# Last stage of a gated mix of long convolution and dilated attention: wider tiles, column groups, and a new order

## The chip, the cores and the metric

One core of a Trainium2 chip runs the program. The metric is device time in microseconds (us), the median of several runs. PE is TensorE, DVE is VectorE, ACT is ScalarE, POOL is GpSimd, SP is the engine that issues most transfers (DMAs).

## The reference, cut to what matters

```python
g = sigmoid((x * gate_w).sum(-1, keepdims=True))        # x = A_q, 2048 rows of 640
kv = short_conv4(A_k, A_shift_k) * A_v
a = x * (long_conv(kv, A_ssm_k) + kv * A_ssm_D)         # causal, length 2048, by FFT
q, k, v = split(x @ B_wqkv)                             # 32 heads of 20
o = softmax over 8 keys at distance 0, 2, ..., 14
out = g * a + (1 - g) * (o @ B_wo)
```

The attention branch works on the same x = A_q. All inputs and the output are bf16.

## The kernel before

Rows are split by parity. x is loaded, transposed on PE (L467) and projected: v (`vproj`, psv, L528) and q, k (`qkproj`, pj, L575) into staging tiles, from which POOL's transfers (`fragger`, L614) build per-group tiles qb, kb of four heads. For each of eight groups of heads PE makes scores (L636), ACT their exponentials (L643), PE the weighted sums O (L664), and DVE divides (L673, L676) into oS. Meanwhile DVE makes the short convolution (`conv`, L481 to L488) and the product with v (L492).

The long convolution is a two-step transform of the kernel h and of u = kv: s1 (`s1_unit`, L697) and s2 (`s2_unit`, L713), in two halves P of 20 + 22 units each in all, with every unit copied out of PSUM by ACT (L284) or DVE (L286). `swaps` (L805, L807) moves halves of h across partitions by DMA into Hw. `products` (L751) multiplies in the transform domain on DVE. `inverse1` (L820) makes 20 units of the first inverse step. `op_tr` (L838) transposes oS, `outproj` (L854) projects it in 16 steps of 128 rows by 640 columns, and the copy out scales it by 1 - g (L858). `load_q` loads x again in the output's layout (L873). `final` does the second inverse step: for each group of three rows t (and a last of one), 32x32 tiles of the matrix T on PE (L893), six ACT copies of 320 scaled by g (L901), then on DVE a multiply by q (L906), an add of the projected attention (L908), and four stores on SP (L911).

The order of all this is set at build time. Each part is a generator that yields requests; a planner (`Plan`) holds a clock for each engine, picks the request with the earliest modelled start plus a weight per part (`PRI`), and chooses ACT or DVE for copies, with leanings (`LEAN_*`). What it picks is issued in that order on each engine; engines run in order and wait on semaphores. Four PSUM slots are shared by all PE work.

Of the kernel before, what the change touches and what calls it, by code (L numbers as in the profile page):

```python
# [17 lines left out]
S = 2048  # L18
# [30 lines left out]
BG = 1266.0  # L49
# [6 lines left out]
def fft_consts():  # L56
# [24 lines left out]
    T = np.tile(T.reshape(32, 64 * 2 * 32), (4, 1))  # L81
# [49 lines left out]
class Req:  # L131


    def __init__(self, engs, cost=0.0, deps=(), take=0, give=(), n=0, move=0.0, pri=None, mode=None, bg=None, mm=0, lean=0.0):
        self.engs, self.cost, self.deps, self.take, self.give, self.n, self.move = engs, cost, deps, take, give, n, move
        self.pri, self.mode, self.bg, self.mm, self.lean = pri, mode, bg, mm, lean
# [4 lines left out]
LEAN_QK = -248.0  # L141
LEAN_V = 87.0
LEAN_H = -137.0
PRI = dict(loads=0, fragger=0, xpose=-9.2, score_gen=-8.6, pv_gen=-5.7, conv=-1.6, conv_v=-24.1, bulk=0, conv_end=0, qkproj=-4.2, vproj=-4.8,
           gate=-0.8, load_G=0, h_slot=0, p2_slot=10.2, u_slot=0, swaps=0, load_T=0, op_tr=4.7, outproj=37.5, load_q=0, products=6.3, final=-18.6,
           h_stream=(-3.7, -4.9), u_stream=(0.9, 2.5), inverse1=(33.7, 30.7))
# [4 lines left out]
class Plan:  # L151


    def __init__(self, nslots):
        self.at = dict(P=0.0, A=0.0, D=0.0, G=0.0, S=0.0, Q=0.0)
# [6 lines left out]
        self.lane = {"S": lane, "Q": lane, "G": []}  # L162
        self.slots = [Bank() for _ in range(nslots)]
        self.streams = []
        self.log = []

    def add(self, gen, pri):
        self.streams.append([pri, gen, next(gen)])
# [6 lines left out]
    def start(self, r, e):  # L175
        t = self.at[e]
        if e == "P" and r.mode != self.mode:
            t += SWITCH
        for d in r.deps:
            if d.t is None:  # L180
                return INF
            t = max(t, d.t + LAT.get((d.eng, e), 60.0))
# [9 lines left out]
    def best(self, r):  # L192
        found = []
        for e in r.engs:
            s = self.start(r, e)
            found.append((s + self.cost(r, e) + (r.lean if e == "A" else 0.0), s, e))
        end, s, e = min(found)
        return s + self.cost(r, e) if s < INF else INF, s, e

    def run(self):  # L200
        while self.streams:
            pick = None
            for k, (pri, gen, r) in enumerate(self.streams):
                end, st, e = self.best(r)
                if st == INF:
                    continue
                p = pri if r.pri is None else r.pri
# [5 lines left out]
            pri, gen, r = self.streams[k]  # L213
# [16 lines left out]
            self.at[e] = end  # L230
# [19 lines left out]
            try:  # L250
                self.streams[k][2] = gen.send(g)
            except StopIteration:
                del self.streams[k]
# [3 lines left out]
def kernel(  # L257
# [45 lines left out]
    g_nat = p0.tile([128, 16], F32, name="g_nat")  # L303
    omg = p0.tile([128, 16], F32, name="omg")
# [62 lines left out]
    def loads():  # L367
# [9 lines left out]
        for c in (1, 0):  # L377
            for q in range(4):
                yield from load(f"k{q}{c}", kin[32 * q:32 * q + 32, 3 + 32 * c:35 + 32 * c, :],
                                raw(k2, 32 * c * D + QC * q, [[64 * D, 32], [D, 32], [1, QC]]), 2000.0)  # L380
        for c in range(2):
            for q in range(4):
                yield from paced(f"v{q}{c}", vin[32 * q:32 * q + 32, c], raw(v2, QC * q + 80 * c, [[64 * D, 32], [D, 64], [1, 80]]), 2100.0)
        yield Req("S", 1.0, [ev("xtr")])
        h_lin = p0.tile([128, 80, 2, 64], BF, name="h_lin", tag="HL")
        st["h_lin"] = h_lin
        for P in range(2):
            for q in range(4):
                for c in range(2):
                    yield from paced(f"h{P}{q}{c}", h_lin[32 * q:32 * q + 32, PL * P:PL * P + PL, c, :],  # L390
                                     raw(A_ssm_k, (160 * q + 80 * c + PL * P) * S, [[64, 32], [S, PL], [1, 64]]), 1200.0)
# [12 lines left out]
    def load_G():  # L404
        yield Req("S", 1.0, [ev("conv"), ev("grow"), ev("vproj")])
# [9 lines left out]
    def load_T():  # L415
        yield Req("S", 1.0, [ev("p2")])
# [3 lines left out]
        yield Req("S", 1.0, [ev("hw1")])  # L420
        T = st["p2"].tile([128, 64, 2, 32], BF, name="T")
        st["T"] = T
        yield from load("T", st["T"][:], cf["T"].ap().rearrange("p (a r b) -> p a r b", a=64, r=2), 2700.0)
# [6 lines left out]
    def heads():  # L430
# [14 lines left out]
        for q in range(4):  # L445
            nc.gpsimd.dma_start(Dz[32 * q:32 * q + 1, :], raw(A_ssm_D, 160 * q, [[0, 1], [1, 160]]))
        for e in range(2):
            masks(e)
            if e == 0:
                for q in range(4):  # L450
                    nc.gpsimd.memset(kin[32 * q:32 * q + 1, 0:3, :], 0.0)
                    nc.gpsimd.dma_start(wraw[32 * q:32 * q + 32].rearrange("p c j -> p (c j)"), raw(A_shift_k, 4 * QC * q, [[0, 32], [1, 4 * QC]]))
        for q in range(4):
            for a, b in ((1, 17), (17, 32)):
                nc.gpsimd.dma_start(kin[32 * q + a:32 * q + b, 0:3, :], raw(k2, (64 * a - 3) * D + QC * q, [[64 * D, b - a], [D, 3], [1, QC]]))
# [59 lines left out]
    def conv_end():  # L515
        g = yield Req("G", 1.0, [ev("convV")])
        mark("conv", g)

    def vproj():
        for n in range(NB):  # L520
# [9 lines left out]
            r = yield Req("AD", n=640, deps=[g.done], give=g.banks, lean=LEAN_V)  # L530
# [5 lines left out]
    def gate():  # L536
# [12 lines left out]
        for gg in range(4):  # L549
            r = yield Req("S", 500.0, [r.done] if gg == 0 else [], move=200.0)  # L550
            nc.sync.dma_start(g_nat[32 * gg:32 * gg + 32, :], raw(src, 64 * (gg % 2) * pt + 16 * (gg // 2), [[32 * pt, 2], [32, 16], [1, 16]]))
        mark("grow", r)
        r = yield Req("D", 500.0, [Ev(r.done.t + 5000.0), ev("conv")])
# [7 lines left out]
    def qkproj():  # L561
        free = [None] * NSTG
        for ft in range(NDT):
            for w in range(2):
# [4 lines left out]
                for k in range(3):  # L569
# [9 lines left out]
                    r = yield Req("AD", n=2 * m, deps=deps, give=g.banks, lean=LEAN_QK)  # L579
# [14 lines left out]
    def fragger():  # L594
# [4 lines left out]
        for ft in range(NDT):  # L599
            for w in range(2):  # L600
                yield Req("G", 1.0, [ev(f"pj{ft}{w}")])
# [84 lines left out]
    def s1_unit(key, P, oc, Am):  # L686
# [14 lines left out]
        e = yield Req("AD", n=1024, deps=[r.done], give=r.banks, lean=LEAN_H if key == "h" else 0.0)  # L701
# [4 lines left out]
    def s2_unit(key, j0, n, Am, deps):  # L706
# [9 lines left out]
        e = yield Req("AD", n=320 * n, deps=[r.done], give=r.banks, lean=LEAN_H if key == "h" else 0.0)  # L716
# [6 lines left out]
    def transform(key, P):  # L723
# [5 lines left out]
        outs = []  # L729
        for j0, n in JS:  # L730
            pdone, edone = yield from s2_unit(key, j0, n, Am, evs)
            outs.append(edone)
            if key == "u":
                todo.append((P, j0, n, edone))
                at(f"todo{len(todo)}", 0.0)
        x = ev(f"{key}s2{P}")
        x.t, x.eng = pdone.t, pdone.eng
        for k, o in enumerate(outs):
            x = ev(f"{key}{P}out{k}")
            x.t, x.eng = o.t, o.eng  # L740

    todo = []

    def products():
        for k in range(2 * len(JS)):
            yield Req("D", 1.0, [ev(f"todo{k + 1}")])
            P, j0, n, edone = todo[k]
            for key in "hw":
                r = yield Req("D", 150.0 + 0.53 * 320 * n, [edone, ev(f"hw{P}")])
                X, U = [st[(x, P)][:].rearrange("p c o (q j) l -> p c (o q) (j l)", j=32)[:, :, :, 4 * j0:4 * j0 + 4 * n] for x in (key, "u")]  # L750
                nc.vector.tensor_tensor(X, U, X, ALU.mult)  # L751
            if k % len(JS) == len(JS) - 1:
                mark(f"mult{P}", r)
# [4 lines left out]
    def h_slot():  # L758
        for P in range(2):
            yield Req("G", 1.0, [ev(f"h{P}{q}{c}") for q in range(4) for c in range(2)])  # L760
            g = yield Req("G", 600.0, [Ev(max(x.t for x in [ev(f"h{P}{q}{c}") for q in range(4) for c in range(2)]) + 6000.0)])
# [4 lines left out]
    def p2_slot():  # L766
        yield Req("G", 1.0, [ev("qk"), ev("gatePE"), ev("frags"), ev("grow")])
# [6 lines left out]
    def h_stream(P):  # L774
        yield Req("G", 1.0, [ev(f"Dz{P}"), ev("p2" if P else "SX")])
        yield from transform("h", P)

    def u_slot():
        yield Req("G", 1.0, [ev("pv"), ev("oS"), ev("p2")])
# [11 lines left out]
    def u_stream(P):  # L791
        yield Req("G", 1.0, [ev("p3"), ev("conv")])
        yield from transform("u", P)

    def swaps():
        for P in range(2):
            yield Req("S", 1.0, outs("h", P) + [ev("p3")] + ([ev("us10"), ev("us11")] if P else []))
# [13 lines left out]
    def inverse1(P):  # L811
        yield Req("G", 1.0, [ev(f"mult{P}")])
# [15 lines left out]
    def op_tr():  # L828
        yield Req("G", 1.0, [ev("oS"), ev("hs10"), ev("hs11")])
# [14 lines left out]
    def outproj():  # L844
        yield Req("G", 1.0, [ev("oTall"), ev("wo"), ev("gate")])
        bl = p0.tile([128, 16, D], BF, name="bl", tag="oS")
        st["bl"] = bl
        wo, oT = st["wo"], st["oT"]
        for t in (*range(4, 16), *range(4)):
            g = yield Req("P", 5 * (215.0 + 56.0), [ev(f"oT{ft}") for ft in range(NDT)], take=1, mode="f", mm=10)  # L850
            op = psum(g, "op", (128, 1024))
            for ft in range(NDT):
                for n0, n1 in ((0, 512), (512, 640)):
                    nc.tensor.matmul(op[:, n0:n1], lhsT=oT[:, ft].rearrange("p h m a -> p a (h m)")[:, t, :], rhs=wo[:, ft, n0:n1],  # L854
                                     start=(ft == 0), stop=(ft == NDT - 1), skip_group_check=True)
            r = yield Req("AD", dict(A=720.0, D=820.0), [g.done], give=g.banks)
            if r.eng == "A":
                nc.scalar.activation(bl[:, t, :], op[:, 0:D], ACT.Copy, scale=omg[:, t:t + 1])  # L858
            else:
                nc.vector.tensor_scalar(bl[:, t, :], op[:, 0:D], omg[:, t:t + 1], None, ALU.mult)  # L860
# [3 lines left out]
    def load_q():  # L864
        yield Req("S", 1.0, [ev(f"{k}s2{P}") for k in "hu" for P in range(2)])
        qg = st["SX"][:, 8192:8192 + 16 * D].rearrange("p (t n) -> p t n", t=16)
        st["qg"] = qg
        for n, (a, b) in enumerate(((4, 16), (0, 4))):
            if n:
                yield Req("S", 1.0, [ev("i10")])  # L870
            for g in range(4):
                r = yield Req("S", 650.0, move=550.0 + 120.0 * (b - a))
                nc.sync.dma_start(qg[32 * g:32 * g + 32, a:b], raw(x2, (32 * (g // 2) + g % 2 + 2 * a) * D, [[64 * D, 32], [2 * D, b - a], [1, D]]))  # L873
            mark(f"qg{a}", r)

    def final():
        yield Req("G", 1.0, [ev("i10")])
        yb2 = st["p2"].tile([128, 2, 3, D], BF, name="yb2")
        ybfree = [Ev(0.0), Ev(0.0)]
# [72 lines left out]
```

## Time and profile before

| | |
|---|---|
| time, median of 3 runs | 248.22 us (247.29 to 249.69) |
| profiled execution: time, span | 247.85 us, 246.1 us |
| PE, PE weight loads | 215.8 us (88%), 167.2 us (68%) |
| DVE, ACT, POOL busy | 185.8, 168.6, 68.8 us |
| L854, outproj | 160 matmuls, 25.7 us busy |
| L858, scaling of the projection | 16 on ACT, 12.7 us, 794 ns each |
| L893, second inverse step | 512 matmuls, 6.6 us busy |
| L901, copies scaled by g | 32 on ACT, 13.8 us, 561 ns each |
| L906, L908 | 6 each on DVE, five of 1,920 elements at 1.16 us |
| T load | 1,024 KB |
| stores | 20 of 120 KB, 4 of 40 KB, on SP |

A line such as `L854 PE MATMUL op<-wo,oT` names the line of the kernel, the engine, the operation and the program's names of output and inputs. Busy time counts what an engine executes, not its waits; matmuls overlap, so the sum of their lengths says less than the distance between their starts. In the 40 slices each digit is tenths of a slice of 6.15 us. "PEclk" is the granted clock of TensorE, 1.00 being full. In the chain, each line is start, length and what ran or was waited for.

### The profile page before, as it was taken

To read this page: it belongs to the slowest core of one execution; us is meant where nothing else is said; L and a number is where in the kernel's file an instruction comes from. 1 tells how busy PE (TensorE), PEld (TensorE's weight loads), DVE (VectorE), ACT (ScalarE), POOL (GpSimd) and SP (SyncE) were. 2 spreads that over 40 slices of the span, in tenths; PEclk is the share of its full clock that TensorE was granted. 3 is DMA by queue.
4 is the path that set the end of the run, shared out by engine and by line. 5 is a ranking of instruction groups with operands and counts; after the bars stand their busy time and mean duration, and the time that the engine had idled before them with its cause. 6 is when DMAs were issued, how large, how long until landed. Compare 5 with 4: busy or idle time off the path is not lost.

```text
span 246.1 us, 8342 instructions
## 1 busy us (share of the span) xinstructions
PE 215.8 (88%) x3654; PEld 167.2 (68%) x3654; DVE 185.8 (76%) x220; ACT 168.6 (69%) x222; POOL 68.8 (28%) x147
## 2 busy tenths in 40 slices
PE   6799999899796999999999999896979999984590
PEld 2699887776464667565766788785867799983350
DVE  1424499999879999978788899995899993134942
ACT  2143543774478785789889799988375589768871
POOL 6699699106719144619000000000000000000000
PEclk9999999999999799995555599999799999999568
DMA  6999965898994959698910000699939910400754
GB/s 230 305 348 192 177 81 137 148 158 142 180 146 95 150 96 138 122 164 245 257 67 4 3 4 3 151 221 212 218 61 204 268 20 3 109 0 5 179 147 107
DMA packets 59580, 33.83 MB, mean 137 GB/s; under 512 B 49212, under 2 KB 56008, under 8 KB 58904
## 3 DMA queue, kind: packets, MB, share of 16 engines
q1 hardware_dynamic: 55192, 27.08, 55.0%
q0 software_dynamic: 3792, 5.81, 10.5%
q8 instruction: 28, 0.46, 0.9%
q10 hardware_dynamic: 560, 0.42, 0.5%
q14 instruction: 8, 0.07, 0.1%
HBM read 20.01 MB, written 2.62 MB: 92 GB/s over the span
## 4 chain that ended last, share of the span: by engine, by line
PE 49%; DMA 13%; POOL 13%; issue 9%; ACT 9%; DVE 4%; SPq 1%; ACTq 0%; POOLq 0%; DVEq 0%
PE op L854 10%; PE pj L575 9%; PE i L820 7%; PE O L664 6%; DMA Hw<-SX 5%; PE sc L636 5%; ACT ETall L643 4%; PE s L713 4%; DMA kb<-stg 3%; POOL qb L614 3%; DMA mm<-ca_mm 3%; DMA KX<-in_A_k_dram 3%; PE psv L528 2%; POOL kb L427 2%; POOL qb L428 2%
## 5 line engine op out<-in xcount | busy, mean ns | idle before, releaser
L643 ACT ACTIVATE ETall<-sc 121x912 bf16<-121x912 f32 (+1 forms) x80 | 63.4, 855 | 12.5 <-PE sc L636 11.6
L575 PE MATMUL pj<-xT,Wqk 128*128 128x342 bf16 (+1 forms) x300 | 49.0, 314 | 1.0 <-ACT ETall L643 0.6
L575 PEld LDWEIGHTS <-Wqk 128*128 128x128 bf16 x300 | 28.4, 98 | 15.8 <-issue 1.4
L481 DVE TENSOR_TENSOR KX<-KX 128x1760 bf16<-128x1760 bf16 (+1 forms) x24 | 27.6, 1161 | 4.3 <-issue 4.0
L614 POOL DMA_DIRECT2D qb<-stg x36 | 18.1, 505 | 36.8 <-PE sc L636 14.6
L528 PE MATMUL psv<-KX,xT 128*121 128x320 bf16 x180 | 27.3, 300 | 1.0 <-DVE xT L286 1.0
L636 PE MATMUL sc<-qb,kb 31*128 31x114 bf16 x576 | 23.4, 241 | 5.4 <-ACT ETall L643 2.0
L284 ACT CAST UC<-s 128x960 bf16<-128x960 f32 (+2 forms) x25 | 22.3, 971 | 7.9 <-PE s L713 6.7
L854 PE MATMUL op<-wo,oT 128*128 128x512 bf16 (+1 forms) x160 | 25.7, 322 | 0.0
L528 PEld LDWEIGHTS <-xT 128*121 128x121 bf16 x180 | 23.4, 134 | 2.2 <-issue 1.2
L713 PEld LDWEIGHTS <-SX 64*128 64x128 bf16 x512 | 19.5, 96 | 7.8 <-issue 7.0
L636 PEld LDWEIGHTS <-kb 31*128 31x128 bf16 x576 | 13.7, 104 | 15.1 <-issue 9.3
L284 ACT CAST stg<-pj 128x684 bf16<-128x684 f32 (+1 forms) x17 | 12.5, 746 | 14.9 <-PE pj L575 9.2
L284 ACT CAST VW<-psv 121x640 bf16<-121x640 f32 x15 | 10.4, 696 | 17.8 <-PE psv L528 17.8
L854 PEld LDWEIGHTS <-oT 128*128 128x128 bf16 x160 | 17.1, 150 | 7.4 <-issue 2.3
L286 DVE CAST UC<-s 128x1024 bf16<-128x1024 f32 (+1 forms) x17 | 19.5, 1195 | 0.0
L488 DVE TENSOR_TENSOR KX<-KX 128x1760 bf16<-128x1760 bf16 (+1 forms) x18 | 18.8, 1042 | 0.3
L614 POOL DMA_DIRECT2D kb<-stg x36 | 17.9, 505 | 3.4 <-ACT stg L284 2.9
L858 ACT ACTIVATE bl<-op,omg 128x640 bf16<-128x640 f32 x16 | 12.7, 794 | 8.6 <-PE op L854 8.6
L820 PE MATMUL i<-F,Hw 128*128 128x128 bf16 x160 | 18.3, 219 | 0.0
L286 DVE COPY xT<-tx 128x1280 bf16<-128x1280 bf16 x8 | 6.5, 824 | 15.6 <-PE tx L467 15.6
L664 PEld LDWEIGHTS <-ETall 121*128 121x128 bf16 x576 | 16.5, 100 | 2.5 <-issue 1.7
(73 smaller groups left out, 376.4 us busy)
## 6 DMA issues: line engine op xcount, KB each, us to landing
xn<-in_A_q_dram SPq DMA_DIRECT2D x8, 320.0 KB, 8.0
KX<-in_A_k_dram SPq DMA_DIRECT2D x8, 320.0 KB, 11.8
vin<-in_A_v_dram SPq DMA_DIRECT2D x8, 320.0 KB, 7.1
h_lin<-in_A_ssm_k_dram SPq DMA_DIRECT2D x16, 160.0 KB, 4.9
Hw<-SX SPq DMA_DIRECT2D x4, 640.0 KB, 7.8
Hw<-Hs SPq DMA_DIRECT2D x4, 640.0 KB, 11.9
out_dram<-SX SPq DMA_DIRECT2D x20, 120.0 KB, 2.2
kb<-stg POOLq DMA_DIRECT2D x28, 85.1 KB, 3.6
```

The costliest lines, as they stand in the source:

```text
L284: nc.scalar.copy(dst, src)
L286: nc.vector.tensor_copy(dst, src)
L481: eng.tensor_tensor(d, kin[:, n + 3 - j:n + 3 - j + m, :], w.to_broadcast([128, m, QC]), ALU.mult)
L528: nc.tensor.matmul(ps[0:BK, n0 // 320, 0:320], lhsT=xT[:, dt, s0:s0 + BK], rhs=Wv[:, dt, n0:n1], start=(dt == 0), stop=(dt == NDT - 1))
L575: nc.tensor.matmul(ps[:, i, 0:n], lhsT=Wqk[:, dt, w, 128 * ft:128 * ft + 128], rhs=xT[:, dt, s0:s0 + n], start=(dt == 0), stop=(dt == NDT ...
L614: nc.gpsimd.dma_start(dst[r0:r0 + rows, 0:wd], stg[fa - f0:fb - f0, 0:wd])
L636: nc.tensor.matmul(sc[:, hh, BQ * bb:BQ * bb + BQ], lhsT=kb[r:r + DH + NF, BK * b:BK * b + 128], rhs=qb[r:r + DH + NF, BQ * b:BQ * b + BQ] ...
L643: nc.scalar.activation(ETall[0:BK, e, :, 0:BQ * nb], sc[0:BK, :, 0:BQ * nb], ACT.Exp, scale=SCALE)
L664: nc.tensor.matmul(O[:, (b - b0) // 6, c0:c0 + 21], lhsT=ETall[0:BK, e, hh, BQ * bb:BQ * bb + 128], rhs=VW[0:BK, b, 4 * t + h4, :], start= ...
L713: nc.tensor.matmul(ps[:, c, 160 * jj:160 * jj + 160], lhsT=st["G"][rows, j0 + jj, rr, :], rhs=Am[rows, rr].rearrange("p o (q j) l -> p j ( ...
L820: nc.tensor.matmul(d, lhsT=st[(key, P)][:, c, o + il // 4, :, il % 4], rhs=M[:, k, :], start=(k == 0), stop=(k == 1), skip_group_check=True)
L854: nc.tensor.matmul(op[:, n0:n1], lhsT=oT[:, ft].rearrange("p h m a -> p a (h m)")[:, t, :], rhs=wo[:, ft, n0:n1], start=(ft == 0), stop=(f ...
```

## The change

The last stage. T becomes block-diagonal for two residues e, so that one 64x64 tile does what four 32x32 tiles did: 256 matmuls instead of 512, and a T of 2,048 KB. The layout of the output tile becomes 32 half rows (320 columns) instead of 16 rows, with the channel quarters ordered 0, 320, 160, 480 (`CH`) in all loads that use them. The output projection is made in four column groups of 32 output rows, N = 320, two t at a time: 640 matmuls instead of 160. Its scaling by 1 - g is two ACT operations or one DVE operation; in the built order it is always ACT. q is multiplied by g on DVE in six operations (`gate_q`), after which ACT copies the second inverse step without a scale, one copy of 960 for a group. There are 11 groups, four copies of the buffer yb in memory that SX has freed, and 26 stores in pieces of 6, 3 and 2 half rows, the last group's second two on ACT's queue.

The planner. Placeholders that took no engine time move to a stream of their own ("Z"); weights and leanings become tables by segment of each part; the two halves of products become two streams; BG, the allowed backlog of paced loads, goes from 1266 to 1665. In the order that comes out, two of the 18 value projections move ahead of the first scores; copies of v move from ACT to DVE early on, staging copies from DVE to ACT later; the gate's matmuls move from the fourth to the first group of scores; seven first-step units of h stand inside or before the fifth group of scores instead of one behind it; DVE's 44 products follow all of its copies of the transforms.

```diff
-    T = np.tile(T.reshape(32, 64 * 2 * 32), (4, 1))
+    Td = np.zeros((2, 2, 32, 64, 2, 2, 32))
+    for e in range(2):
+        Td[:, e, :, :, :, e, :] = T
+    T = Td.reshape(128, 64 * 2 * 64)
...
-        for t in (*range(4, 16), *range(4)):
-            g = yield Req("P", 5 * (215.0 + 56.0), [ev(f"oT{ft}") for ft in range(NDT)], take=1, mode="f", mm=10)
...
-                for n0, n1 in ((0, 512), (512, 640)):
-                    nc.tensor.matmul(op[:, n0:n1], lhsT=oT[:, ft].rearrange("p h m a -> p a (h m)")[:, t, :], rhs=wo[:, ft, n0:n1],
+        for t in (*range(8, 32, 2), *range(0, 8, 2)):
+            g = yield Req("P", 40 * 33.3 + 60.0, [ev(f"oT{ft}") for ft in range(NDT)], take=1, mode="g", mm=40)
...
+                            c = 64 * e + 32 * w
+                            nc.tensor.matmul(op[c:c + 32, tt, 0:320], lhsT=oT[:, ft, h, 32 * e:32 * e + 32, a], rhs=wo[:, ft, 320 * w:320 * w + 320],
+                                             start=(ft == 0), stop=(ft == NDT - 1), tile_position=(0, c), skip_group_check=True)
...
+    def gate_q():
+        for a, b in ((8, 14), (14, 20), (20, 26), (26, 32), (0, 4), (4, 8)):
+            r = yield Req("D", 150.0 + 0.53 * 320 * (b - a), [ev("ql0" if a < 8 else "ql8"), ev("gate")])
+            reg = st["qg"][:, a:b, :]
+            nc.vector.tensor_tensor(reg, reg, g_nat[:, a:b].unsqueeze(2).to_broadcast([128, b - a, 320]), ALU.mult)
...
-        for n, (t0, m) in enumerate(((4, 3), (7, 3), (10, 3), (13, 3), (0, 3), (3, 1))):
+        for n, (t0, m) in enumerate([(t, 3) for t in range(8, 32, 3)] + [(0, 3), (3, 3), (6, 2)]):
...
-                            nc.tensor.matmul(pss[q // 2][32 * gg:32 * gg + 32, q % 2, 160 * tt:160 * tt + 160], lhsT=T[rows, n2, r, :],
+                            nc.tensor.matmul(ps[64 * e:64 * e + 64, qp, 160 * tt:160 * tt + 160], lhsT=T[rows, n2, r, :],
...
-                    nc.scalar.activation(yb[:, tt, 320 * k:320 * k + 320].rearrange("p (q c) -> p q c", q=2),
-                                         pss[k][:, :, 160 * tt:160 * tt + 160], ACT.Copy, scale=g_nat[:, t0 + tt:t0 + tt + 1])
+            nc.scalar.copy(yb[:, 0:m, :].rearrange("p t (q c) -> p q t c", q=2), ps[:, :, 0:160 * m].rearrange("p q (t c) -> p q t c", t=m))
...
-    def products():
+    def products(P):
```

More of the change, by code (lines that the diff above doesn't have):

```diff
@@ L48 @@
 WARM = 8
-BG = 1266.0
+CH = [0, 320, 160, 480]
+BG = 1665.0
 def _np_bf16(a):
@@ L200, in run @@
     def run(self):
-        while self.streams:
+        while any(s[2] is not None for s in self.streams):
             pick = None
-            for k, (pri, gen, r) in enumerate(self.streams):
-                end, st, e = self.best(r)
+            for k, s in enumerate(self.streams):
+                if s[2] is None:
+                    continue
+                end, st, e = self.best(s[2], self.lean(k), s[4])
                 if st == INF:
                     continue
-                p = pri if r.pri is None else r.pri
+                p = self.pri(k)
                 key = (st + 120.0 * p, p, k)
@@ L914 @@
+            a = t0 - 3 if n < 8 else t0
+            reg = st["qg"][:, a:t0 + m, :]
+            for e in range(2):
+                for w in range(2):
+                    (nc.scalar if w and n == 10 else nc.sync).dma_start(raw(outf, (e + 2 * a) * D + 320 * w, [[64 * D, 32], [2 * D, t0 + m - a], [1, 320]]),
+                                                            reg[64 * e + 32 * w:64 * e + 32 * w + 32])
     heads()
     for gen in (loads, fragger, xpose, score_gen, pv_gen, conv, bulk, conv_v, conv_end, qkproj, vproj, gate, load_G, h_slot, p2_slot,
-                u_slot, swaps, load_T, op_tr, outproj, load_q, products, final):
```

233 lines of the change are left out of this document (121 added, 112 removed), and 8 rows, old and new, of the table PRI.

## The prediction

> **What bounds the kernel now.** I read the slices first, then busy time in windows of 6 us, then the chain of waits, then the groups by line.
>
> ```profile
> PE   6799999899796999999999999896979999984590
> DVE  1424499999879999978788899995899993134942
> ACT  2143543774478785789889799988375589768871
> ...
> PEclk9999999999999799995555599999799999999568
> ```
>
> PE is busy nearly everywhere, so its share says little. VectorE (DVE) is full from about 30 to 104 us and from 138 to 205 us; ScalarE (ACT) is fuller than PE in the score stage. The stages, by the timeline: start to 101.7 us (projections, the shifted convolution of k on DVE); to 137.7, where the last exponential of the scores ends; to 183.5, where the last second-step matmul of u ends; to 219.8, output projection and first inverse step; the rest is the last stage.
>
> ```profile
> core 0: us, PE busy (x) PEld busy (x) DVE busy (x) ACT busy (x) POOL busy (x), PEclk, DMA share, GB/s
> 150.00:156.00 6.00, 5.32 (x125) 4.66 (x121) 6.00 (x7) 5.74 (x8) 0.00 (x0) 1.00 0.08 18
> ...
> 168.00:174.00 6.00, 3.90 (x86) 3.45 (x85) 3.32 (x4) 3.35 (x5) 0.00 (x0) 0.91 1.01 213
> ...
> 222.00:228.00 6.00, 2.42 (x192) 1.68 (x174) 2.85 (x3) 5.76 (x14) 0.00 (x0) 0.96 0.05 11
> 228.00:234.00 6.00, 3.50 (x187) 2.28 (x188) 5.58 (x6) 5.23 (x13) 0.00 (x0) 0.50 0.74 187
> ```
>
> Between 138 and 183 us both copying engines are full: the stage is as long as the copies out of PSUM, shared by two engines, except at 168 to 174, where all three engines fall to about 3.4 of 6. The list of waits names the cause:
>
> ```profile
> DVE SX L751 <- DMA Hw<-SX: 2.7, 1, 2.7
> ```
>
> A product (L751) stands on DVE ahead of copies and waits for the swap DMA. In the last stage (222 to 234) ACT is full and PE is not. Its chain:
>
> ```profile
> 220.91 1.67 PE i L893 x168
> 222.58 1.78 issue
> ...
> 226.06 2.61 ACT yb L901 x6
> ...
> 230.67 1.70 issue
> ...
> 233.21 5.09 PE op L854 x20
> ...
> 238.58 1.56 PE op L854 x10
> ...
> 240.17 0.80 ACT bl L858
> ...
> 240.99 0.49 DVE SX L908
> ```
>
> Six scaled copies (L901) take 2.61 us for each group of three rows; two output projections take 5.09 us at clock 0.50 and the third 1.56 us at full clock. "issue" is PE without instructions: 128 matmuls, 256 instructions, lie between the ends of successive such waits (224.36, 228.09, 232.37), and the queue of instructions carries 28 packets, 0.46 MB, which is 261 of PE's 7,308 instructions each. So one packet arrives per 3.7 to 4.3 us at best.
>
> **The change, part by part.** Times are positions in the profiled execution: span 246.1 us, time 247.85, so 1.75 lie outside the span; the median of the three runs is 248.22, 0.37 above this execution. I take the order of each engine from the two programs.
>
> *Order, to the last exponential.* Two value projections (1.36 us each) move ahead of the first scores, which start about 45.5 instead of 42.8, but the same work leaves the next stretch. The second staging fragments no longer hold PE at 64.5 (waits of 0.83 and 0.43): five projections and the gate, about 8 us, now stand between. DVE loses two value copies (0.74 pace) and one staging copy (0.8), so the convolution's last multiply ends near 100.4 instead of 104.5. Six more first-step units of h enter the fifth score group. One of their copies is on ACT, between exponentials, and needs the convolution finished (it reuses its memory): ACT reaches it near 96.6 and waits to 100.4, with the fifth group's remaining exponentials behind it. After the wait, ACT has 11 exponentials, copies and stagings, about 9.5 us, before the sixth group: 110 against 110.7. The last three groups have the same order as before. Step: -0.7, bounds -5 (all PE idling before 110 gone, which is 5.2) and +5 (that wait of 3.8 added whole, plus a late h load).
>
> *Last exponential to output projection.* Before: 18 of 20 first-step units of h are copied out now, 12 then; 71 copies remain instead of 77, and products follow all of DVE's copies, so none waits in front of them for a swap. ACT's share is 13 copies of 1024 at 0.93 (6.51 us for 7), 25 of 960 at 0.89 (6.22 for 7), 3 of 640 at 0.69: 36.4 us. DVE's is 9 at 1.14, 16 of 960 or 640, 5 transposes at 1.14, one softmax division: 33.7. ACT was 93% busy from 138 to 168, so 39.1 us, against 45.8 from 137.7 to 183.5. Step: -6.7, bounds -9 (no idling) and 0 (the same idling again).
>
> *Output projection in column groups.* Before: ten matmuls (N 512 and 128) take 1.41 us per 128 rows. After: forty of N=320, each on 32 columns of the array, four at a time. The gate is the row of this form:
>
> ```profile
> 97.52 1.26 PE L542 MATMUL gps<-xT,wgz 128*32 128x512 bf16 x20
> 98.72 0.46 PE L575 MATMUL pj<-xT,Wqk 128*128 128x342 bf16 x2
> ```
>
> The columns are start and length; the next matmuls begin at 98.72, so it is 60 ns per matmul. The projections L575 take 0.43 ns per column (ten of 342 start to start in 1.47 us); 512 columns, four matmuls at a time, would be 55, so 5 ns are left over. N=320 is then 34 + 5 = 39 ns, about 1.6 us per group of forty. The lower bound is 1.41. Eleven groups remain after u's last matmul, 17.6 us; they consume 80 instructions per 1.6 us, 5.1 us per packet, while 4 MB of q and of the doubled matrix T load. One packet under load in this trace came after 174.5 and was usable at 182.69, with 1.39 us of issue wait. I add one such wait: 19.0. The first inverse step stays at 17.9 (3.57 per 64 matmuls, 320 of them). Total 36.9 against 36.3: +0.6, bounds -3 and +6. DVE's 44 products (0.57 pace, 24.8) end 22 us into this, before their first use at 28.
>
> *Gate on DVE.* Two multiplications of 1280 and four of 1920 per partition, bf16 by a broadcast f32. All-bf16 L908 takes 1.16 for 1920; f32 copies (960 in 1.15, 640 in 0.81) extrapolate to 2.17 and 1.49. L676 has a broadcast f32 operand too, and its 480 in 0.65 lie on the slow line, so I take 8.7 + 3.0 us; the fast end is 6.4 less in all. The Trainium skill ("VectorE: DVE Perf Modes", "What auto-detection actually checks") says two elements per cycle need every tensor to be 16-bit; by it the slow price holds and the fast end goes. The four large ones stand in DVE's queue ahead of the copies of the 17th and 19th inverse units, which the last stage needs.
>
> *Last stage.* With the steps above the projection starts at 176.0, the tenth inverse unit is made at 204.0 and copied by 205.1, four gates run to 213.8, the two late copies to 216.1 (PE finished at 212.9 and waits), two gates to 219.1. Then eleven pairs of multiply and add at 0.57 each (0.41 for the short ones): 231.1 is DVE's earliest end. PE needs 24 matmuls a group instead of 96; ACT one copy of 960, 0.89, instead of 2.61. But four projections, not three, are left in this stage behind nine groups: PE gets slots for the first two near 222.6, and at half clock, as before, they take 5.1; then 0.4, about 2, 0.4, 1.6 to 2.5, the scaling 0.87 and an add: 233.4. From 212.9 that is 20.5 against 21.6 (219.8 to 241.5): -1.1; at full clock -3.4; bounds -6 and +3.
>
> *Stores.* 241.5 to the end took 4.6 us for 24 issues, eight of them after 240.3. Now six follow the second-last add, two on ACT: about 4.1. Step: -0.5, bounds -1.5 and +3 (640-byte rows instead of 1,280 move more slowly; output leaves DVE at 480 KB per 2.3 us, 209 GB/s, near the 187 to 237 seen).
>
> T's second megabyte costs 5 us of DMA at about 205 GB/s (186 to 198 us) and is hidden: q and T end some 20 us after 176, T is needed at 216. Moving the loads and dropped placeholders of the planner issues nothing.
>
> Sum: -0.7 - 6.7 + 0.6 - 1.1 - 0.5 = -8.4; 247.85 - 8.4 = 239.4 us.
>
> **The rivals.** *Better, about 234.* The gates run at the bf16 rate, or the clock stays up at the end: 3 to 5.5 us less. For: the second-step matmuls kept clock 1.00 with gaps. Against: 228 to 234 at 0.50.
>
> *Instructions late, about 245.* Packets under load take 8.2 us each, as the one at 182.69. In 20 us of loading 2.4 packets arrive, 620 of 880 instructions; the rest takes 5 us: 25 instead of 19, and everything behind moves by 6. Against: others under load were used without a wait.
>
> *Scores late, about 246.* ACT's wait for the convolution grows and the next groups do not catch up: +7. For: ACT is 88% busy from 108 to 138.
>
> *The other side, about 254.* Weight loads of the four column groups do not hide behind matmuls. Now 640 instead of 160 of them, strided; L854's loads average 150 ns where others have about 98. If each of the forty exposes 27 to 40 ns (17.1 us busy for 160 loads is 107 per 128 columns, 27 per 32), a group takes 40 x (34 + 27 to 40), 2.4 to 3.0 us: 15 groups times 0.8 to 1.4, +12 to +21. It decides from 2.2 us per group, where 15 x 0.56 eats 8.4. Against: the gate's 60 ns holds at most 5 of exposure. The Trainium skill ("TensorE: Matmul & The Clock Gate", "What overlaps and what doesn't") says that a weight load overlaps running matmuls only if its row group differs, and these four share all rows; by that rule this rival comes true, and the gate's row so far contradicts it.
>
> **How the numbers follow.** Forecast (235.5 to 243) 0.50; better 0.22; instructions late 0.12; scores late 0.08; other side 0.08. About 1% (245.7 to 250.7) is what a measurement of this kernel can tell. Faster: 0.50 + 0.22 + 0.09 of the third + 0.03 of the fourth = 0.84. Slower: 0.07 of the last. The rest, 0.09, is within 1%. The range 231 to 247 takes in the second and most of the third and fourth, and leaves 0.08 above for the other side and some 0.08 for both tails.
>
> **What would show it.** Right: the last exponential near 137; no L751-like product waiting for the swap; 39 us to the projections; a group of forty at 1.6 us; gates at 2.17 us with PE idle about 3 us before the last stage; two projections at half clock near the end. Wrong: gates near 1.16, issue waits of 2 us and more inside the projections, groups above 2.2 us, or an ACT wait over 6 us before 104.

## The result and the profile after

| | before | after |
|---|---|---|
| time, median | 248.53 us (247.29 to 249.69, 4 runs) | 262.71 us (259.74 to 263.78, 4 runs) |
| profiled execution: time, span | 247.85, 246.1 us | 262.99, 261.2 us |

The changed kernel is slower: 1.053 times the time before (95% interval 1.042 to 1.064). The forecast was 239.4, its range ended at 247. Lengths of the stages in us, from the two profiled executions; the column of the forecast is the prediction's:

| stage | before | forecast | after |
|---|---|---|---|
| start to the last exponential | 137.7 | 137.0 | 148.1 |
| to the projections (last second step of u) | 45.8 | 39.1 | 39.2 |
| projections and first inverse step | 36.3 | 36.9 | 46.4 |
| to the last add | 21.7 | 20.5 | 19.5 |
| to the end of the span | 4.6 | 4.1 | 8.0 |

Two steps came as forecast, three did not. Executions of one order differ by up to 3 us in a stage (up to the first scores even more: with the changed order the first exponential lies between 43.0 and 48.4), so single differences below that prove little. The profiled executions of experiments 6 and 7 were slow ones; of these two only the times are used.

The slices of the changed kernel, 6.53 us each:

```profile
PE   7799978999769979999799999999974299976920
DVE  1566999999867989977888799998999900799970
ACT  1011332785538886598898799987952229776940
PEclk9999997999979998999655579999999959999985
```

PE's hole is no longer at 168 to 174 but in the 31st and 32nd slice (196 to 209), with the clock at half behind it; DVE is empty in the 33rd and 34th. The windows of 6 us (columns as in the prediction):

```profile
166.00:172.00 6.00, 5.35 (x132) 4.66 (x128) 5.99 (x7) 5.57 (x7) 0.00 (x0) 1.00 0.98 221
...
196.00:202.00 6.00, 2.65 (x80) 2.65 (x84) 6.00 (x12) 1.71 (x4) 0.00 (x0) 1.00 1.21 186
202.00:208.00 6.00, 1.93 (x60) 1.63 (x48) 6.00 (x12) 2.07 (x5) 0.00 (x0) 0.98 1.12 328
208.00:214.00 6.00, 5.44 (x84) 3.52 (x88) 0.55 (x2) 0.94 (x2) 0.00 (x0) 0.50 0.17 68
...
238.00:244.00 6.00, 4.73 (x193) 4.04 (x188) 5.86 (x10) 5.70 (x8) 0.00 (x0) 1.00 0.12 27
```

At 166 DVE is full: no product waits there for a swap any more. From 196 to 208 PE works 38% of the time, while the DMA engines are full. From 238 on DVE is the bound, and the clock stays at 1.00, where half was forecast. The timeline of PE in the projections (start, length, what, idle before it):

```profile
187.29 2.53 PE L883 MATMUL op<-wo,oT 128*32 128x320 bf16 x67
190.96 4.58 PE L883 MATMUL op<-wo,oT 128*32 128x320 bf16 x128 [1.14 <-issue]
199.35 4.58 PE L883 MATMUL op<-wo,oT 128*32 128x320 bf16 x128 [3.81 <-issue]
208.56 7.20 PE L883 MATMUL op<-wo,oT 128*32 128x320 bf16 x117 [4.63 <-issue]
```

128 matmuls are 256 instructions, one packet. They take 4.58 us, 34.0 ns from one start to the next, but the waits end 8.4 and 9.2 us apart, and after the last one the clock is 0.50 from 208 to 214. The trace's records of the instruction queue bear out that packets are what PE waits for: packets of 16 KB land at 189.42, 198.01 and 207.34, and each wait ends 1.2 to 1.5 us behind one of them.

### The profile page after: what moved, and what is told of

Read it like the earlier page. It is cut to its first block, busy times and chain, and to the rows that moved or that the text cites. A ratio compares the mean times of both kernels' runs of the same rounds, so it can differ in the third digit from the quotient of the medians.

```text
span 261.2 us, 8815 instructions
## 1 busy us (share of the span) xinstructions
PE 216.9 (83%) x3878; PEld 173.4 (66%) x3878; DVE 206.5 (79%) x239; ACT 162.7 (62%) x214; POOL 69.4 (27%) x147
## 4 chain that ended last, share of the span: by engine, by line
DVE 33%; PE 29%; issue 12%; DMA 8%; ACT 8%; SPq 4%; POOL 2%; DVEq 0%; POOLq 0%; ACTq 0%
PE op L883 7%; DVE KX L516 7%; DVE KX L523 5%; PE pj L611 5%; SPq L391 4%; ACT ETall L679 4%; DVE UC L321 4%; PE s L733 4%; DVE SX L910 4%; PE O L700 4%; PE i L845 3%; PE sc L672 3%; DMA xn<-in_A_q_dram 3%; DMA KX<-in_A_k_dram 3%; DVE Hs L321 3%
## 5 line engine op out<-in xcount | busy, mean ns | idle before, releaser
L611 PE MATMUL pj<-xT,Wqk 128*128 128x342 bf16 (+1 forms) x300 | 50.8, 321 | 3.5 <-DVE stg L321 3.0
L611 PEld LDWEIGHTS <-Wqk 128*128 128x128 bf16 x300 | 28.5, 100 | 19.1 <-issue 3.1
L319 ACT CAST stg<-pj 128x684 bf16<-128x684 f32 (+1 forms) x22 | 16.5, 748 | 33.8 <-PE pj L611 33.8
L883 PE MATMUL op<-wo,oT 128*32 128x320 bf16 x640 | 26.6, 325 | 10.0 <-issue 9.6
L883 PEld LDWEIGHTS <-oT 128*32 128x32 bf16 x640 | 22.4, 143 | 13.5 <-issue 10.7
L319 ACT CAST UC<-s 128x960 bf16<-128x960 f32 (+2 forms) x27 | 24.4, 980 | 2.8 <-PE s L733 1.5
L516 DVE TENSOR_TENSOR KX<-KX 128x1760 bf16<-128x1760 bf16 (+1 forms) x24 | 24.6, 1043 | 1.8 <-DMA g_nat<-KX 1.4
L888 ACT ACTIVATE bl<-op,omg 128x320 bf16<-128x320 f32 x32 | 15.1, 546 | 16.9 <-PE op L883 16.9
L749 PEld LDWEIGHTS <-SX 64*128 64x128 bf16 x512 | 19.5, 95 | 3.7 <-issue 3.1
L321 DVE CAST Hs<-s 128x1024 bf16<-128x1024 f32 (+2 forms) x17 | 19.2, 1165 | 1.1 <-PE s L733 0.7
L523 DVE TENSOR_TENSOR KX<-KX 128x1760 bf16<-128x1760 bf16 (+1 forms) x18 | 18.8, 1045 | 0.5
L845 PEld LDWEIGHTS <-Hw 128*128 128x128 bf16 x160 | 17.9, 114 | 0.0
L700 PE MATMUL O<-VW,ETall 121*128 121x21 bf16 x576 | 17.5, 176 | 0.2
```

The source lines that it names most:

```text
L319: nc.scalar.copy(dst, src)
L321: nc.vector.tensor_copy(dst, src)
L516: eng.tensor_tensor(d, kin[:, n + 3 - j:n + 3 - j + m, :], w.to_broadcast([128, m, QC]), ALU.mult)
L523: eng.tensor_tensor(ta if j else dst, ta, tb, ALU.add)
L611: nc.tensor.matmul(ps[:, i, 0:n], lhsT=Wqk[:, dt, w, 128 * ft:128 * ft + 128], rhs=xT[:, dt, s0:s0 + n], start=(dt == 0), stop=(dt == NDT ...
L700: nc.tensor.matmul(O[:, (b - b0) // 6, c0:c0 + 21], lhsT=ETall[0:BK, e, hh, BQ * bb:BQ * bb + 128], rhs=VW[0:BK, b, 4 * t + h4, :], start= ...
```

## The experiments

All times are medians beside runs of the kernel before on the same chip; the ratio is to these. "Stage" lengths are from the profiled execution. The changed kernel's own ratio is 1.042 to 1.064; the times of 6, 7, 9 and 12 are clear of it, and the other edits are read by their stages.

**1. The taps' copy on ACT.** In the changed kernel one small copy on DVE, the next in line before the convolution, lasts from 27.23 to 36.09. The first fence is DVE, the second POOL at that time:

```profile
26.48 0.83 DVE L321 CAST VW<-psv 121x640 bf16<-121x640 f32 x1 [0.53 <-PE psv L563]
27.23 8.83 DVE L531 COPY KX<-KX 128x640 bf16<-128x640 bf16 x1
36.09 2.06 DVE L516 TENSOR_TENSOR KX<-KX 128x1760 bf16<-128x1760 bf16 x2
```

```profile
27.52 2.01 POOL L462 COPY kb<-mm 128x2178 bf16<-128x2178 bf16 x1
29.46 1.90 POOL L463 COPY qb<-mm 128x2052 bf16<-128x2052 bf16 x1
31.30 1.81 POOL L433 MEMSET ETall<- 128x2048 bf16 x1
33.04 2.66 POOL L434 MEMSET VW<- 128x576 bf16 x1
35.76 0.62 POOL L436 MEMSET VW<- 7x32 bf16 x2
```

Before, the same copy (L496) took 0.48 us, ahead of POOL's block:

```profile
23.81 0.48 DVE L496 COPY KX<-KX 128x640 bf16<-128x640 bf16 x1
```

```diff
-        yield Req("D", 800.0, [ev("k01")])
-        nc.vector.tensor_copy(wl, wraw.rearrange("p c j -> p j c"))
+        yield Req("A", 700.0, [ev("k01")])
+        nc.scalar.copy(wl, wraw.rearrange("p c j -> p j c"))
```

> The copy of the convolution's taps (640 elements, 8.83 us on DVE between 27.2 and 36.1, while POOL copies and clears) goes to ACT; nothing else moves. Theory (the DVE copy is held up by POOL, and the value copies and PE behind it): the first multiply starts near 28.5 instead of 36.1, but two or three multiplies then take 2 to 3 us each beside POOL, so the convolution runs 3 to 5 us ahead; first scores near 44 instead of 47.3, the last exponential 2 to 5 us earlier, time 258 to 261. Rival (this delay is absorbed later, the loss of 10.4 us up to the last exponential comes from the staging copies behind the convolution at 66 to 104): the first scores move, the last exponential stays within 1 us of 148, time 262 to 263.

261.41 us, 1.047 (1.038 to 1.056). The first scores came at 42.2, 5 us earlier, and the last exponential at 149.0: the rival, though the time lies below its 262. The third group of scores starts at 84.5, against 84.1 in the changed kernel, so the gain was gone by then. DVE lost it at 65, in the list of waits of this run:

```profile
DVE KX L516 <- DMA g_nat<-KX: 6.5, 1, 6.5
```

**2. The order of before.** The planner gets the old weights, leanings and backlog (constant tables, BG 1266).

> The planner gets the weights, leanings and backlog of the kernel before; the last stage, its layout, T, gates and stores stay those of the changed kernel. The order on every engine is then that of before up to the output projection. Theory (the order lost 10.4 us up to the last exponential): the last exponential is at 137.7 and the output projection starts near 183.5, as before; from there on, long issue waits under the loads as in the changed kernel, 26 to 29 us for the projections, time 256 to 260. Rival (the new order of the channel quarters and the new layout cost the time upstream): the last exponential stays near 148, and with the old order's 45.8 us behind it the time is about 268.

266.61 us, 1.067 (1.060 to 1.075). The last exponential is at 139.4, as the theory has it; u ends 46.2 us later, as before. So the order cost these 9 us, not the layout. The projections took 18.0 us, not 26 to 29: only nine groups stand there instead of eleven, with one issue wait of 3.51. The total missed the expectation too: gates and three scalings now stand on DVE between the pairs of multiply and add, and the last add comes 30.3 us behind the inverse step instead of 19.5.

**3. and 4. Loads out of the projections.** T early; then also q held until ten projection groups are scaled.

```diff
-        yield Req("Z", 0.0, [ev("hw1")])
+        yield Req("Z", 0.0, [ev("p3")])
         T = st["p2"].tile([128, 64, 2, 64], BF, name="T")
...
+            if not n:
+                r = yield Req("G", 200.0, [ev("bl26")])
+                nc.gpsimd.tensor_copy(qg[:, a, 0:1], st["bl"][:, 26, 0:1])
...
```

> The load of T (2 MB) is issued ahead of the swaps, near 150, instead of behind q's; all else is the same. Theory (packets of instructions come late because q and T, 4.6 MB, load during the projections): only 2.5 MB load there, one of the two waits of about 4 us goes, and with it some of the time at half clock: the projections take 21 to 25 us instead of 28.5, time 256 to 260. Rival (the packets cannot come faster than the column groups use them, or the groups themselves are slow): 28 us still, time 262 to 263.

> As the run with T early, and q's load is held by a one-element copy on POOL until ten of the sixteen projection groups have been scaled, so nothing loads during most of them. Theory (loads make the packets late): no issue wait above 1.5 us in the projections, full clock, 18 to 20 us instead of 28.5; the first inverse step runs beside q's load and may pay 1 to 2 us; time 253 to 256. Rival (the column groups need packets faster than they come at all): 12 groups are 960 instructions, 3.75 packets, which at 3.7 to 4.3 us each would bind only at 14 to 16 us; so if 25 us or more remain, the groups themselves are slow, and the time stays at 260 or more.

260.85 us, 1.046 (1.039 to 1.053), and 260.79 us, 1.043 (1.034 to 1.051). The projections take 23.9 and 19.8 us instead of 28.5, as the theory said, with the same matmuls in the same order; the groups are not slow, their packets were. (Other executions with T and q loading together have 25.4 to 27.0, so the first gain is not sure in its size.) In 4 one issue wait of 2.71 us stayed, more than the 1.5 expected, while the transfers of the swaps were still under way. Both times missed their ranges. Of the second gain nothing reached the end: the gates started at 224.7 when q had landed, and the last stage began 7.2 us behind the inverse step instead of 3.0.

**5. and 6. Plain transfers of the gate's rows,** then with the taps on ACT.

```diff
-            nc.sync.dma_start(g_nat[32 * gg:32 * gg + 32, :], raw(src, 64 * (gg // 2) * pt, [[32 * pt, 2], [32, 16], [1, 32]]))
+            for k in range(2):
+                nc.sync.dma_start(g_nat[32 * gg + 16 * k:32 * gg + 16 * k + 16, :],
+                                  raw(src, (64 * (gg // 2) + 32 * k) * pt, [[pt, 1], [32, 16], [1, 32]]))
```

> The gate's rows are read out of KX by eight transfers of one partition each instead of four that step over 32 partitions; the order on all engines stays. The stepping form covers all of KX, so the convolution's multiply waits for it on DVE, since the gate now stands in the first score group; with the plain form the wait is gone. Theory (this wait and the staging copies behind it): in the changed kernel DVE stands 1.4 us at 72 and PE 2.8 us behind the staging copy; 2 to 4 us less up to the last exponential (144 to 146), time 258 to 261. Rival (the staging copies wait for the fragments of their buffer, whatever the convolution does): the last exponential stays within 1 us of 148, time 262 to 263.

> The plain form of the gate's transfers and the taps' copy on ACT together. In the run with the taps on ACT alone, DVE stood 6.5 us for the gate's transfer, which gave back the 5.2 us won before. Theory (the two hide each other): the first scores near 42.5, no wait of DVE for g_nat, the convolution ends near 103 instead of 110, the last exponential between 139 and 143, time 253 to 257. Rival (a third wait, staging copies behind fragments, takes it back): the last exponential at 146 or later, time 260 or more.

259.32 us, 1.035 (1.028 to 1.042), and 259.42 us, 1.035 (1.029 to 1.041). The wait for g_nat is gone from DVE's list, the last exponential at 146.7; but a run whose order up to there was the unchanged one (experiment 8) has 146.7 too, so in time this wait is not shown to count by itself. Over all runs with the changed order that are read by stages the last exponential lies at 143.9 to 146.7 with the plain form (5, 9, 10, 12) and at 146.7 to 149.5 without it; but in 10 and 12 the small copy also missed POOL's block. The second edit adds nothing to the time, which stays above the theory's 253 to 257.

**7. Gates ahead of the copies; 8. the last stores on two queues.**

```diff
-    "gate_q": (3, (63.1, 49.1), (0, 0)),
+    "gate_q": (3, (20.0, 49.1), (0, 0)),
```

```diff
+                    if w and n > 7:
+                        late.append((e, w, a, t0 + m, reg))
+                        continue
...
+        for e, w, a, b, reg in late:
+            nc.scalar.dma_start(...)
```

> The planner's weight of the gates is lowered, so that all six stand on DVE right behind the products, ahead of the copies of the inverse step; two of these copies go to ACT; all else stays. In the changed kernel DVE has nothing to do from 208.5 to 223.1 and the gates then keep two copies waiting, PE 3.0 us. Theory: four gates run from 208.5 to 217, the last two when q's second load has landed near 229, PE goes from the first to the second inverse step without the 3 us, time 258 to 260. Rival (the last two gates wait for that load and keep the copies as late as before): the gap of 3 us stays, time 262 to 263.

> Of the last three groups' stores the second half of the columns goes to ACT's queue, behind ACT's last copy: 4 + 2 on ACT, 20 on SP. Theory (SP issues one store in 0.48 us and is 2.5 us of adds behind at the end, eight stores start after 254.8): the time from the last add to the end falls from 8.0 to about 5 us, time 259 to 260. Rival (what is waited for is the transfers of 640-byte rows themselves): 7 to 8 us stay, time 262 to 263.

258.09 us, 1.028 (1.021 to 1.036): as the theory says. 260.52 us, 1.045 (1.037 to 1.053): from the last add to the end 6.8 us instead of 8.0, between theory and rival; SP still issues its last store 3.6 us behind the last add.

**9. The sum of 3, 5, 7 and 8.**

> Four of the single edits together on the changed kernel: plain transfers of the gate's rows, T loaded early, the six gates ahead of the copies, the last stores on two queues. Theory (each removes a wait of its own): their measured parts add up, 1.5 us up to the last exponential, 4.6 in the projections, 2 before and in the last stage, 1.3 behind the last add, so the time is 252 to 255. Rival (one wait takes the place of the other): 256 or more.

252.25 us, 1.011 (1.002 to 1.020): the time is in the theory's range. The parts are not those expected: 2.8 us up to the last exponential (1.5 expected), 2.6 in the projections (4.6), 2.5 in the last stage (2), 2.1 behind the last add (1.3). PE now passes from the first to the second inverse step in 1.4 us instead of 3.0; 5.9 us to the end. The projections still take 25.9.

**10. q one load at a time, held on POOL; 11. the same with the old order up to the last exponential; 12. held on ACT.** Each large load of q waits for a one-element copy out of the second, fourth, sixth and eighth scaled group:

```diff
             for g in range(4):
+                d = []
+                if not n:
+                    t = 10 + 4 * g
+                    r = yield Req("G", 200.0, [ev(f"bl{t}")])
+                    nc.gpsimd.tensor_copy(qg[32 * g:32 * g + 32, a, 0:1], st["bl"][32 * g:32 * g + 32, t, 0:1])
+                    d = [r.done]
```

In 12 the two lines are `Req("A", 250.0, ...)` and `nc.scalar.copy(...)`.

> As the sum, and the four large loads of q are each held by a one-element copy on POOL until the second, fourth, sixth and eighth group of projections has been scaled, so that one load of 480 KB at a time is under way. Theory (a packet of instructions waits behind all that is queued ahead of it, 8 to 10 us with four loads issued at once): the projections take 19.5 to 21.5 us instead of about 24, the gates start by 212, time 249 to 252. Rival (what counts is that something loads at all, not how much is queued): 23 to 25 us remain, and with the later end of q's load the time is 253 or more.

> As the run with paced q, and up to the last exponential the weights and leanings of the kernel before (for the projections, the convolution, the scores and the first steps of h); behind it the changed kernel's own. Theory (the changed order loses up to the last exponential and gains behind it, because no product waits there for a swap): last exponential at 138 to 140, 41 to 43 us from there to the projections, which start at 180 to 183; projections 20, inverse 18, last add 16 to 17 later, 7 to the end; time 243 to 248. Rival (what the changed order gains behind the last exponential is only the work it did earlier): 45 to 46 us as before, time 249 to 251.

> As the run with paced q, but the four one-element copies that hold q's loads are on ACT, between the scalings, instead of on POOL, where they ended only when DVE's products ended, so that all of q loaded after 205. Theory (a packet waits behind what is queued ahead of it): one load of 480 KB at a time, issued every 2.7 us; the projections take 19.5 to 21.5 us against 25.9 in the sum, q's first 24 rows are there by 205, the gates run from 206 to 217, last add at 238 to 240, time 245 to 249. Rival (what counts is that something loads, not how much is queued): the projections take 23 us or more, time 250 to 253.

10: 258.89 us, 1.037 (1.028 to 1.046); 11: 256.96 us, 1.036 (1.027 to 1.044). Neither tested what it was meant to. POOL's four tiny copies did not end before DVE's products did (the first alone lasted from 186.46 to 205.04), so all of q loaded after 205 and the gates waited until 218.9. POOL's timeline in 10:

```profile
186.46 19.30 POOL L908 COPY SX<-bl 32x1 bf16<-32x1 bf16 x4 [61.46 <-ACT bl L890]
```

The front part of 11 can be read all the same: last exponential 141.3, 43.2 us from there to the projections at 184.5; in 10, with the changed order, 143.9 and 39.9, at 183.7. Before: 183.5.

12: 249.03 us (12 runs), 0.997 (0.991 to 1.002): no difference from the kernel before, at the upper edge of the theory's 245 to 249. The projections take 20.6 us, in the theory's range, with loads still under way:

```profile
184.71 2.54 PE L885 MATMUL op<-wo,oT 128*32 128x320 bf16 x67
190.01 10.42 PE L885 MATMUL op<-wo,oT 128*32 128x320 bf16 x256 [2.76 <-issue]
201.03 4.29 PE L885 MATMUL op<-wo,oT 128*32 128x320 bf16 x117 [0.60 <-issue]
```

Against before, stage by stage: +8.0 to the last exponential, -6.7 to the projections, +3.3 in projections and inverse step, -4.7 to the last add, +1.3 to the end.

## Why the prediction was wrong

**Output projection in column groups: the step that failed most (+0.6 forecast, +10.1 measured).** The matmuls were cheaper than forecast, 1.36 us per forty against 1.6, and the rival of exposed weight loads is out: 34.0 ns from one start to the next are what the prediction counts for the columns alone. The rule that the Trainium skill states ("TensorE: Matmul & The Clock Gate", "What overlaps and what doesn't"), weight loads overlapping only across row groups, would make it 2.4 us or more by the prediction's estimate; the trace differs. What failed is the term for instructions: "I add one such wait" of 1.4. There were three, 9.6 us together, and behind the last about 3 us more at half clock. The prediction's own figures had it: the groups use up a packet in 5.1 us, and the one under load had taken 8.2. Its rival, "Instructions late", drew this conclusion and got 0.12; waits that end 8.4 and 9.2 us apart bear it out, and it too left out the clock.

T's load, "hidden" because T is needed late, was not: not by its end but by its place beside the packets. With T and q loading together the instruction queue has two late packets in a row, 7.9 to 9.7 us from start to start (changed kernel, 1, 5, 8); with T early it has one, 9.3 us (3 and 9), and the third wait, which was 1.05 to 4.63 us, is gone. In the length of the projections this is less clear: 28.5, 25.7, 27.0 and 25.4 us against 23.9 and 25.9. With the same 2 MB of q one load at a time the packets start 5.2 to 6.0 us apart, and the projections take 20.6 (12). With neither q nor T under way it is 3.7 to 5.0 us, and 19.8, 17.9 and 19.5 (4, 10, 11); there one wait of 2.5 to 2.7 us is left, the first, beside the transfers of the swaps. In all these runs a packet itself takes 0.9 to 1.5 us; what is late is its start. So the loads delay the packets, and q's one at a time much less than four at once. Whether it is the depth of the queue or the share of the DMA engines taken (from 190 to 196 it was 1.04 in the changed kernel, 0.56 in 12), these runs do not separate.

**Order, to the last exponential (-0.7 forecast, +10.4 measured).** By the first exponentials of the first six of the eight groups, ACT's timeline has 43.5, 65.0, 76.1, 86.6, 102.5, 111.2 before, and 47.8, 69.8, 84.1, 93.8, 108.7, 121.9 after. So 4.3 us are lost at the start, 6.2 by the fifth group and 10.7 by the sixth. At the start DVE's small copy ran into POOL's block. That is a matter of tenths: in experiments 10 and 12, with the same order there, it started at 26.17 and 25.85 and took 0.48 us; in 5 and 9 at 26.37 and 26.36, and took 8.96 and 8.72. And experiment 1 shows that an earlier start alone is not what sets the end.

The step that failed is where the prediction puts the fifth group. It lets ACT reach a copy of h there at 96.6 and pass it at 100.4, when the convolution would be done. Measured, the convolution's product with v ends at 110.0 (104.6 before) and this copy starts at 110.6. From there to the sixth group the forecast has 9.5 us of ACT's work, and it took 11.4. Without POOL's block and the wait for the gate's transfer (10 and 12) the fifth group starts at 103.0 and 104.1, so these two have a share in its lateness; no run separates them.

The fifth group itself takes 13.3 us instead of 8.7, in every run with this order 13.2 or more, and 8.7 in the two with the old one. PE's timeline there, before and after:

```profile
102.07 1.67 PE L575 MATMUL pj<-xT,Wqk 128*128 128x349 bf16 x10
...
104.27 1.65 PE L575 MATMUL pj<-xT,Wqk 128*128 128x349 bf16 x10 [0.20 <-ACT ETall L643]
...
106.20 1.67 PE L575 MATMUL pj<-xT,Wqk 128*128 128x349 bf16 x10
...
109.72 0.51 PE L697 MATMUL s<-F,h_lin 64*128 64x128 bf16 x8
```

```profile
108.25 1.62 PE L611 MATMUL pj<-xT,Wqk 128*128 128x342 bf16 x10
...
110.12 0.62 PE L733 MATMUL s<-F,h_lin 64*128 64x128 bf16 x16
110.69 1.65 PE L611 MATMUL pj<-xT,Wqk 128*128 128x349 bf16 x10
112.27 0.40 PE L733 MATMUL s<-F,h_lin 64*128 64x128 bf16 x8
...
115.21 1.67 PE L611 MATMUL pj<-xT,Wqk 128*128 128x349 bf16 x10
...
118.29 1.66 PE L611 MATMUL pj<-xT,Wqk 128*128 128x349 bf16 x10
```

Four projections and seven units of h, where the old order has three and one: from start to start that is 1.6 + 6 x 0.33 = 3.6 us more on PE. ACT has more too: four staging copies and one copy of h, which the old order makes on DVE or outside the group. The window of the group, before and after (columns as in the prediction):

```profile
102.46:111.16 8.70, 7.95 (x149) 5.30 (x148) 6.89 (x11) 7.83 (x11) 2.99 (x11) 1.00 1.03 163
108.66:121.93 13.27, 12.43 (x218) 8.34 (x217) 9.95 (x13) 11.58 (x16) 4.79 (x12) 1.00 0.61 197
```

PE's busy time grows by 4.5 us and ACT's by 3.8, and both are near full in both orders, so the runs do not tell which of the two sets the group's length. I had looked for ACT's wait for the convolution ("Scores late") and counted ACT's copies, but put the work of the moved units on PE nowhere.

**Last exponential to the projections (-6.7 forecast, -6.6 measured).** Right in size and in the missing wait for the swap. But most of it was not won: experiments 10 and 11 have 39.9 and 43.2 us, and both reach the projections at 184. The changed order pays in the fifth group what it saves here; only some 2.6 us (45.8 to 43.2, one execution each) remain for the products' place.

**Gate on DVE: right.** 8.35 us for four and 2.89 for two. The rule that the prediction cites from the Trainium skill ("VectorE: DVE Perf Modes", "What auto-detection actually checks"), two elements per cycle only with 16-bit tensors throughout, agrees: 2.09 us per 1,920 against the 1.16 of all-bf16. The operand is also one value repeated along the row, and no run separates the two. The two copies did wait behind the gates, PE 3.0 us. That DVE would stand idle from 208.6 to 223.1, ahead of the gates, I had not seen; experiments 7 and 9 put the gates there.

**Last stage (-1.1 forecast, -2.2 measured).** The two projections at half clock did not come: the clock was 1.00. DVE's pairs were the bound, at 1.27 us, not 1.14: 22 operations from 239.3 to 253.2.

**Stores (-0.5 forecast, +3.4 measured), beyond the bound of +3.** There are 28 stores, 26 of them on SP. SP issues one in 0.48 us; the last three groups bring ten of its 26 within 2.4 us, and SP also stood 2.1 us behind an earlier store. Eight were issued from 254.8 on, when all adds were done. With four of them moved to ACT this stretch is 5.6 to 6.8 us (experiments 8 to 12), against 7.7 to 8.1 without (the changed kernel, 1, 3, 4, 5), so the queue is a part of it; the rest I have not separated from the transfers.

What stays open: why SP waited those 2.1 us, what sets the start of the fourth group, between 88.6 and 95.5 in these runs (86.6 before), and why the clock halves after one wait (4.63 us) and not after another (3.81); it is not the length alone, for it halved with a wait of 1.93 us in experiment 1 and with one of 2.76 in 12.

## What to carry to other kernels

Work that an order moves forward has to be charged where it arrives; the stage it leaves is only half of the sum. A large load that nobody needs soon is not free while PE runs many short matmuls: its instructions come through the same DMA engines, so issue such loads early or one at a time, and hold them on an engine that is not blocked. A transfer that steps over partitions can be ordered against a whole tile: the one that read two partitions 32 apart held a DVE multiply on the same tile, 6.5 us in experiment 1, and with one partition per transfer the wait was gone. That order comes from the program's semaphores.

## What the runs showed of the hardware

- DVE and POOL stop each other for long. One DVE copy of 640 elements took 8.83 us beside POOL's copies and clears. It took 0.48 where it was over before POOL's block began (start 26.17 against 26.77, experiment 10), and 8.96 where it was not (26.37 against 26.75, experiment 5). The other way round, the first of POOL's four copies of one element took 18.6 us beside 34 of DVE's products, and the next three 0.2 each. The Trainium skill ("SBUF — State Buffer", "Who interferes with whom") says that the ports which DVE and GpSimd share are held for a whole instruction while the other engine blocks; the trace agrees, and shows that the wait can span four long instructions of POOL and over thirty of DVE.
- Matmuls on 32 columns each, in four column groups, with N = 320, keep a pace of 34.0 ns from start to start, weight loads of 32 columns included.
- A packet of PE's instructions is 16 KB, 256 instructions. With nothing large loading the packets start 3.7 to 4.4 us apart (experiment 10), with T and four loads of q under way 8.5 and 9.7 us (the changed kernel), and each takes 0.9 to 1.5 us itself.
